# The remainder of 48 gated features as 32 and 16 rows in four row groups, and the last store on ScalarE's queue

## The chip, the core and the metric

The kernel runs on one core of a Trainium2 chip. The metric is the device time of one execution in microseconds (us). Five engines work in parallel and meet at semaphores: TensorE (PE in the profile; its weight loads are shown apart as PEld), VectorE (DVE), ScalarE (ACT), GpSimd (POOL) and SyncE (SP). SP, ACT and POOL also give out DMA transfers; each gives out its own in order, and an instruction that waits holds up all that is behind it on the same engine.

## What is computed

A layer-normed input feeds two branches, whose results are added to the input (S = 2048 tokens, D = 512, bf16):

```python
xn = layernorm(x)
# A: sliding window of 8 keys, two apart, 32 heads of 16
q, k, v = split(xn @ wqkv)
A = (softmax(q . k[s - 2 w] / 4 + mask) @ v) @ wo
# B: gated by a mix over the tokens, Fh = 688
z  = gelu(xn @ w_in);  z1, z2 = z[:, :688], layernorm(z[:, 688:])
g  = w_sp @ z2 + b_sp
B  = (z1 * g) @ w_out
out = x + A + B
```

The change concerns the last product, `(z1 * g) @ w_out`, which sums over 688 = 5 x 128 + 48 features, and how it shares TensorE with `... @ wo`.

## The kernel before

Tokens are cut into 16 tiles of 128, and into two halves `th` of 8 tiles. The order of work is written out by hand in two lists, `ten` (TensorE and ScalarE) and `vec` (VectorE), and a small function walks them and issues each step as soon as the steps that it needs have been issued. In these lists `M<j>` is the mix of tile j (`mix_tile`, matmuls on L378, moved out of PSUM by ScalarE on L381), `g<j>` its gate, `a<th>.<n>` a step of attention on VectorE (L351, L355, L364), `O<n>` a load of output weights, `X<th>` a load of the residual, `Q0`, `Q2`, `Q3` the output matmuls, and `F<n>` the end of a group of tiles.

**The gate.** `gate(j)` (L385) multiplies the mixed tile by `z1` on VectorE (L386) and gives out DMA transposes on SP's queue, which put the features on the partitions, in `uT`: chunks 0 to 4 are full, chunk 5 holds the remaining 48. Tiles whose `j // 2` is even take one transpose (L390), and the 48 rows land on partitions 0 to 47. The other tiles take two (L392, L393), the second so placed that the 48 rows land on partitions 64 to 111.

**The output matmuls.** TensorE can use its 128 rows as one group, as two of 64, or as four of 32, and matmuls in different groups can run at the same time; `tile_position=(row, 0)` picks the group. Tiles are grouped by four: group 0 is tiles 0, 2, 4, 6, group 1 is 1, 3, 5, 7, and 2 and 3 are the same for the second half. For each tile three kinds of matmul add up in one PSUM bank:

- `gated_full` (L417): five matmuls on all 128 rows.
- `gated_rest` (L423): one matmul of 48 rows, in the row group of 64 at row 0 or 64, so that neighbouring tiles of a group run in pairs.
- `attention_out` (L429; in the last group L566): for each of 16 head dimensions, four matmuls of 32 rows in the row groups 0, 32, 64 and 96, one for each tile of the group.

`out_pair` (Q0) does groups 0 and 1: full, rest, rest, attention, attention, full. `out_group(2)` (Q2) does full, rest, attention. `out_last(3)` (Q3) does attention, rest, full, and there the last tile is computed in two column halves in two banks, so that one half can be moved out while the other is computed.

**The end.** `finish` (L432) adds the residual on VectorE (L434) and stores the tile from SP's queue (L435). The two halves of tile 15 make the last two stores. `finish_pair` does two tiles with one store (L442).

**Loads in ScalarE's queue.** `load_wout` (L404, step O4) gives out three DMAs: the five full chunks of `w_out` (L405), and its last 48 rows twice, for partitions 0 and 64 (L407). `load_wo` (L402) loads `wo` in four steps. `load_res` (L410) loads the residual, that of the second half on SP, behind the transposes of tile 15.

Of the kernel before, what the change touches and what calls it, by code (L numbers as in the profile page):

```python
# [7 lines left out]
BF16 = mybir.dt.bfloat16  # L8
# [5 lines left out]
P = 128  # L14
S = 2048
D = 512
# [8 lines left out]
HS = S // 2  # L25
GS = HS // 4
FH = 688
F = 2 * FH
FHALF = FH // 2
MF = FH // P  # L30
FREST = FH - MF * P
# [7 lines left out]
def kernel(  # L39
# [14 lines left out]
    A = nc.scalar  # L54
    G = nc.gpsimd
    PE = nc.tensor
    SP = nc.sync
# [36 lines left out]
    qk_r = [sb.tile([P, QKH], BF16, name=f"qk{t}") for t in range(2)]  # L94
    qk = [r[:].rearrange("p (a c s) -> p a c s", a=2, c=C) for r in qk_r]
    uT = [r[:, 0:(MF + 1) * HS].rearrange("p (m s) -> p m s", m=MF + 1) for r in qk_r]
    gs = [qk_r[0][:, (MF + 1) * HS + n * FH:(MF + 1) * HS + (n + 1) * FH] for n in range(3)]
    prod = [sb.tile([P, 2 * C * HS], BF16, name=f"prod{n}")[:] for n in range(2)]
    z2_r = sb.tile([P, NT * FH], BF16, name="z2")
# [285 lines left out]
    def gate(j, g):  # L385
        V.tensor_tensor(z1u[:, j, 0:FH], g, z1u[:, j, 0:FH], ALU.mult)  # L386
        th, t0 = j // 8, (j % 8) * P

        if j // 2 % 2 == 0:
            SP.dma_start_transpose(uT[th][:, :, t0:t0 + P], z1u[:, j, :])  # L390
        else:
            SP.dma_start_transpose(uT[th][:, 0:MF, t0:t0 + P], z1u[:, j, 0:MF * P])  # L392
            SP.dma_start_transpose(uT[th][:, MF, t0:t0 + P], z1u[:, j, MF * P - 64:MF * P + 64])  # L393

    def idle(n, k=1):

# [6 lines left out]

    def load_wout():  # L404
        A.dma_start(wout[:, 0:MF, :], B_w_out[0:MF * P, :].rearrange("(m p) n -> p m n", p=P))  # L405
        for r in (0, 64):
            A.dma_start(wout[r:r + FREST, MF, :], B_w_out[MF * P:FH, :])  # L407

    def load_res(th):
        (SP if th else A).dma_start(xr[th], x2[th * HS:(th + 1) * HS, :].rearrange("(i p) d -> p i d", p=P))  # L410
# [5 lines left out]
        for m in range(MF):  # L416
            PE.matmul(po[:, cols], uT[th][:, m, t0:t0 + P], wout[:, m, cols], start=(start and m == 0), stop=(stop and m == MF - 1))  # L417

    def gated_rest(tiles, start, stop, bank=None, cols=slice(0, D)):
        for i in tiles:  # L420
            r, t0 = 64 * (i // 2 % 2), (i % 8) * P
            b = po[i] if bank is None else bank
            PE.matmul(b[:, cols], uT[i // 8][r:r + FREST, MF, t0:t0 + P], wout[r:r + FREST, MF, cols],  # L423
                      start=start, stop=stop, tile_position=(r, 0))

    def attention_out(th, s, pos, start, stop):
        for d in range(DH):
# [1 line left out]
                PE.matmul(pos[g], op[32 * g:32 * g + 32, th, d, s * P:(s + 1) * P], wo_r[32 * g:32 * g + 32, d, :],  # L429
                          start=(start and d == 0), stop=(stop and d == DH - 1), tile_position=(32 * g, 0))  # L430

    def finish(i, po, cols=slice(0, D)):  # L432
        o = nxt("ot", ot)
        V.tensor_tensor(o[:, cols], po[:, cols], xr[i // 8][:, i % 8, cols], ALU.add)  # L434
        SP.dma_start(out2[i * P:(i + 1) * P, cols], o[:, cols])  # L435

    def finish_pair(i):

# [10 lines left out]
    for i in range(5, NT):  # L449
# [4 lines left out]
        p01 p02 zs8 m10 zn8 zn9 zn10 zn11 p03 W1 f10 zs12 p10 zn12 zn13 zn14 zn15  # L454
        m11 d11 x0 m12 g0 d12 p11 u0 g1 m13 p12 W2 W3 f13 p13 c0 g2
        a0.0 a0.1 g3 x1 a0.2 a0.3 g4 a0.4 g5 a0.5 a0.6 a0.7 g6 u1 a0.8 g7 a0.9 g8 a0.10 g9 a0.11 c1 g10
        a1.0 a1.1 g11 a1.2 a1.3 g12 a1.4 g13 a1.5 g14 a1.6 a1.7 g15 X1 a1.8 a1.9 F0 a1.10 a1.11 F1 F2
    """.split()
    ten = """
        T0 T1 B GL z0 z1 h0 T3 h1 z2 h2 z3 h3 LZ k00 k01 q0 k02 q1 k03 q2 z4 h4 z5 q3 h5 k10 k12 k11 k13  # L460
# [75 lines left out]
    def out_pair():  # L536

        first, second = groups[0], groups[1]
        for i in first:
            gated_full(i, po[i], True, False)  # L540
        gated_rest(first, False, False)
        gated_rest(second, True, False)
        attention_out(0, 0, [po[i] for i in first], False, True)
        attention_out(0, 1, [po[i] for i in second], False, False)
        for i in second:
            gated_full(i, po[i], False, True)

    def out_group(n):
        tiles = groups[n]
        for i in tiles:  # L550
            gated_full(i, po[i], True, False)
        gated_rest(tiles, False, False)
        attention_out(n // 2, n % 2, [po[i] for i in tiles], False, True)

    def out_last(n):

        tiles = groups[n]
        th, s, last = n // 2, n % 2, tiles[-1]
        hb = [po[last], po[groups[n - 1][0]]]
        cols = [slice(0, D // 2), slice(D // 2, D)]  # L560
        for d in range(DH):
            for g in range(4):
                a = slice(32 * g, 32 * g + 32)
                for dd, b, c in [(d, po[tiles[g]], slice(0, D))] if g < 3 else \
                        [(2 * d % DH + x, hb[d // 8], cols[d // 8]) for x in range(2)]:
                    PE.matmul(b[:, c], op[a, th, dd, s * P:(s + 1) * P], wo_r[a, dd, c],  # L566
                              start=(dd == 0), stop=False, tile_position=(32 * g, 0))
        gated_rest(tiles[:3], False, False)
        for b, c in zip(hb, cols):
            gated_rest([last], False, False, b, c)  # L570
        for i in tiles[:3]:
            gated_full(i, po[i], False, True)
            finish(i, po[i])
        for b, c in zip(hb, cols):
            gated_full(last, b, False, True, c)
            finish(last, b, c)

    gates, done = {}, set()
    at = [attend(0), attend(1)]
# [1 line left out]
    def do(n):  # L581
        k, a = n[0], n[1:]
        i = int(a) if a.isdigit() else 0
        th, w2 = (int(a[0]), int(a[1])) if len(a) == 2 and a.isdigit() else (i, 0)
        if k == "T":
            turn_pe(i)
            if i == 0:
                idle(1)
        elif n[:2] == "zs":
            z2_stats(int(n[2:]), 4)  # L590
        elif n[:2] == "zn":
            z2_norm(int(n[2:]), False)
        elif n == "z0":

            gates["z0"], gates["z1"] = nxt("mm", mm), nxt("mm", mm)
            for t, hh in ((0, 0), (1, 0), (0, 1)):
                z_half(t, 1, gates[f"z{t}"], hh)
        elif n == "z1":
            turn_pe(2)
            z_half(1, 1, gates["z1"], 1)  # L600
        elif k == "z":
            gates[n] = z_part(i, 1)
        elif k == "h":
            z2_gelu(i, gates[f"z{i}"])
        elif k == "q":
            z2_square(i)
        elif k == "k":
            qk_chunks(th, w2 // 2, w2 % 2)
        elif k == "v":
            v_pair(i)  # L610
        elif k == "H":
            v_halo()
        elif k == "S":
            head_sum(th, w2)
        elif k == "B":

            pb = mm[2][:, 1, :].bitcast(BF16)[:, 0:NT]
            PE.transpose(pb, b16[:], ident[0:NT, 0:NT])
            A.copy(b_col[:], pb)
        elif k == "y":  # L620
            z1_tile(i)
        elif k == "M":
            gates[i] = mix_tile(i)
        elif k == "W":
            load_wsp(i)
        elif k == "O":
            load_wo(i) if i < 4 else load_wout()
        elif k == "X":
            load_res(i)
        elif n == "GL":  # L630
            A.preload_act_table(ACT.Gelu_apprx_tanh)
        elif n[:2] == "EG":
            A.preload_act_table(ACT.Gelu_apprx_tanh)
        elif n[:2] == "EL":
            A.preload_act_table_set("natural_log_exp_and_others")
        elif k == "Q":
            [out_pair, None, lambda: out_group(2), lambda: out_last(3)][i]()
        elif k == "F":
            tiles = groups[i]
            for t in (0, 2):  # L640
                if (i, t) in ((0, 0), (0, 2), (1, 0)):
                    finish_pair(tiles[t])
                else:
                    finish(tiles[t], po[tiles[t]])
                    finish(tiles[t + 1], po[tiles[t + 1]])
        elif k == "e":
            softmax_exp(i)
        elif k == "i":
            softmax_inv(i)
        elif k == "s":  # L650
            ln_stats(i)
        elif k == "R":
            ln_root_act(i, 1)
        elif k == "V":
            ln_inv(i)
        elif n == "LE":
            load_early()
        elif k == "r":
            ln_root(i, 1)
        elif k == "n":  # L660
            ln_norm(i)
        elif k == "t":
            turn_dma(i)
        elif n == "LZ":
            load_x(12, 4, A)
        elif n == "LX":
            load_tokens()
        elif n == "LW":
            load_weights()
        elif k == "m":  # L670
            run(prod_ops(th, w2)[0])
        elif k == "j":
            run(prod_ops(th, w2)[1])
        elif k == "f":
            prod_ops(th, w2)[2]()
        elif k == "p":
            prod_ops(th, w2)[3]()
        elif k == "d":
            fold_dma(th, w2)
        elif k == "K":  # L680
            k_halo()
        elif k == "x":
            run(softmax_max(i))
        elif k == "u":
            run(softmax_sum(i))
        elif k == "c":
            run(softmax_scale(i))
        elif k == "g":
            gate(i, gates[i])
        elif k == "a":  # L690
            at[int(a[0])][int(a[2:])]()
        done.add(n)
# [53 lines left out]
```

## Time and profile before

| | us |
|---|---|
| median of three runs (201.41, 201.60, 201.67) | 201.6 |
| the profiled execution, its own time | 201.44 |
| its span in the trace | 199.7 |
| PE busy | 195.2 (98%) |
| DVE busy | 175.7 (88%) |
| ACT busy | 95.0 (48%) |
| POOL busy | 39.0 (20%) |

All durations below are from the one profiled execution. Its span is 1.7 us shorter than its time; the difference lies outside the trace. PE's share is high in any case, because matmuls are pipelined and their recorded ends are modelled: what counts is the distance from the start of one matmul to the start of the next. The output stage starts at 162.7 us; VectorE's last work ends at 196.98 us. The granted clock of TensorE is full in all slices of the span.

### The profile page before, as it was taken

Reading aid. Unit: us, or ns where it says so; the run is one execution under the profiler, and the core shown is the slowest. Engines: PE = TensorE matmul, PEld = TensorE weight load, DVE = VectorE, ACT = ScalarE, POOL = GpSimd, SP = SyncE. Lnnn points to the kernel's source line nnn. Section 1 sums busy time; section 2 is a strip of 40 time slices with the busy share of each in tenths; the row PEclk is TensorE's granted clock in tenths of the full one; section 3 lists DMA queues with packets and bytes.
Section 4 is the critical chain, followed back from the end, with each engine's and each line's share of the span. In section 5 each row is a group of like instructions: output and inputs, shape, how many; then the busy total and the mean of one; then the engine's idle time right before and its main releaser. Section 6 shows DMA issues by size and latency. Waiting matters only on the chain.

```text
span 199.7 us, 3843 instructions
## 1 busy us (share of the span) xinstructions
PE 195.2 (98%) x1587; PEld 119.0 (60%) x1587; DVE 175.7 (88%) x192; ACT 95.0 (48%) x149; POOL 39.0 (20%) x62
## 2 busy tenths in 40 slices
PE   7999999999999999999999999999999999999993
PEld 2655555555666666666566666666666654444652
DVE  4899689999889799999999999999999799897333
ACT  3779879899888738886433373312221110000000
POOL 4367540149490421600000000000000000000000
PEclk9999999999999999999999999999999999999999
DMA  6999679599640837898979199996959711712023
GB/s 173 290 261 182 108 161 289 113 199 198 133 83 17 196 62 151 173 112 81 236 173 213 26 266 289 111 278 134 260 101 249 141 43 39 257 61 105 9 99 105
DMA packets 64289, 30.84 MB, mean 154 GB/s; under 512 B 53440, under 2 KB 62512, under 8 KB 64144
## 3 DMA queue, kind: packets, MB, share of 16 engines
q1 hardware_dynamic: 59296, 19.23, 46.1%
q0 software_dynamic: 1904, 6.59, 16.9%
q10 hardware_dynamic: 3072, 4.78, 9.3%
q8 instruction: 12, 0.20, 0.4%
q14 instruction: 5, 0.04, 0.1%
HBM read 10.03 MB, written 2.10 MB: 61 GB/s over the span
## 4 chain that ended last, share of the span: by engine, by line
PE 95%; DVE 1%; DMA 1%; ACT 0%; issue 0%
PE mm L378 37%; PE mm L213 19%; PE mm L258 14%; PE mm L273 7%; PE mm L417 7%; PE mm L429 5%; PE aux L417 2%; PE mm L566 1%; DMA z<-in_A_x_dram 1%; PE mm L423 1%; PE aux L309 1%; DVE stats L186 1%; PE aux L205 0%; PE aux L566 0%; ACT xnT L206 0%; DVE z L434 0%
## 5 line engine op out<-in xcount | busy, mean ns | idle before, releaser
L378 PE MATMUL mm<-z,wsp 128*128 128x344 bf16 x384 | 56.8, 309 | 0.0
L378 PEld LDWEIGHTS <-wsp 128*128 128x128 bf16 x384 | 37.5, 98 | 18.8 <-issue 0.4
L213 PE MATMUL mm<-wts,xnT 128*128 128x344 bf16 x256 | 40.3, 309 | 0.2 <-ACT xnT L206 0.2
L381 ACT ACTIVATE qk<-mm,b_col 128x688 bf16<-128x688 f32 x16 | 13.3, 833 | 49.8 <-PE mm L378 46.0
L351 DVE TENSOR_TENSOR prod<-vp,a_sb 128x4096 bf16<-128x4096 bf16 x16 | 36.0, 2283 | 0.0
L213 PEld LDWEIGHTS <-xnT 128*128 128x128 bf16 x256 | 24.7, 98 | 13.9 <-ACT xnT L206 0.5
L258 PE MATMUL mm<-xnT,wts 128*128 128x512 bf16 x128 | 29.1, 379 | 0.0
L355 DVE TENSOR_TENSOR prod<-prod,prod 128x8192 bf16<-128x8192 bf16 x6 | 26.5, 4419 | 0.1
L293 DVE TENSOR_TENSOR prod<-qk 128x4096 bf16<-128x4096 bf16 (+1 forms) x12 | 22.7, 1930 | 1.4 <-ACT qk L260 1.4
L258 PEld LDWEIGHTS <-wts 128*128 128x128 bf16 x128 | 14.6, 114 | 11.9
L378 PE MATMUL mm<-z,z 128*128 128x344 bf16 x128 | 19.2, 309 | 0.0
L260 ACT CAST qk<-mm 128x1024 bf16<-128x1024 f32 x16 | 16.2, 1012 | 4.8 <-PE mm L258 3.8
L378 PEld LDWEIGHTS <-z 128*128 128x128 bf16 x128 | 12.5, 98 | 6.1
L417 PE MATMUL mm<-wts,qk 128*128 128x512 bf16 (+1 forms) x65 | 14.7, 371 | 0.0
L273 PE MATMUL mm<-xnT,wts 128*32 128x512 bf16 x256 | 14.2, 379 | 0.0
L250 ACT ACTIVATE z<-mm 128x688 bf16<-128x688 f32 x16 | 11.8, 744 | 4.5 <-PE mm L213 4.5
L417 PEld LDWEIGHTS <-qk 128*128 128x128 bf16 x85 | 8.1, 98 | 9.2 <-issue 0.6
L186 DVE BATCH_NORM_STATS2 stats<-z 128x6 f32<-128x512 bf16 x16 | 11.0, 685 | 2.0 <-DMA z<-in_A_x_dram 1.9
L224 ACT ACTIVATE z<-mm 128x688 bf16<-128x688 f32 x16 | 11.9, 745 | 1.6 <-PE mm L213 1.6
L229 ACT ACTIVATE z_junk<-z 128x688 bf16<-128x688 bf16 x16 | 12.4, 773 | 0.0
L273 PEld LDWEIGHTS <-wts 128*32 128x32 bf16 x256 | 9.5, 138 | 4.3
L434 DVE TENSOR_TENSOR z<-mm,wsp 128x512 bf16<-128x512 f32 (+1 forms) x7 | 4.3, 649 | 8.0 <-PE mm L429 4.8
(98 smaller groups left out, 210.1 us busy)
## 6 DMA issues: line engine op xcount, KB each, us to landing
prod<-prod POOLq DMA_DIRECT2D x6, 512.0 KB, 5.1
z<-z POOLq DMA_DIRECT2D x4, 512.0 KB, 5.9
wts<-in_A_wo_dram ACTq DMA_DIRECT2D x4, 512.0 KB, 6.0
out_dram<-z SPq DMA_DIRECT2D x9, 128.0 KB, 1.7
z<-in_A_x_dram SPq DMA_DIRECT2D x4, 256.0 KB, 4.3
wts<-in_A_wqkv_dram SPq DMA_DIRECT2D x2, 512.0 KB, 6.6
z<-in_A_x_dram ACTq DMA_DIRECT2D x1, 1024.0 KB, 6.6
wsp<-in_A_x_dram SPq DMA_DIRECT2D x1, 1024.0 KB, 5.6
```

The lines of the kernel that those rows point to most:

```text
L186: V.bn_stats(stats[:, i, :], xs[:, i, :])
L213: PE.matmul(pz[:, hh, 0:FHALF], xnT[:, kc, i * P:(i + 1) * P], w_z2[:, hh, kc] if part else w_z1[:, kc, hh * FHALF:(hh + 1) * FHALF], star ...
L229: A.activation(z2_junk[:], z2[:, i, :], ACT.Square, accum_out=zsq[:, i:i + 1])
L258: PE.matmul(pq[:, cc, :], w_c[:, kc], xnT[:, kc, t0:t0 + D], start=(kc == 0), stop=(kc == C - 1))
L260: A.copy(qk[b // 2][:, a, 2 * c2:2 * c2 + 2, o:o + D], pq[:])
L273: PE.matmul(pv[32 * g:32 * g + 32, dd, :], w, r, start=(kc == 0), stop=(kc == C - 1), tile_position=(0, 32 * g))
L293: ops.append(lambda ww=ww, k=k, c=c: V.tensor_tensor(pr[:, ww, c], q[:, c], k[:, c], ALU.mult))
L351: return lambda: V.tensor_tensor(dst, vp[:, :, th, off:off + GS], a_sb[:, th, w].unsqueeze(1).broadcast_to([P, DH, GS]), ALU.mult)
L355: return lambda: V.tensor_tensor(dst, dst, x, ALU.add)
L378: PE.matmul(pg[:, hh, 0:FHALF], w[:, k, (j % 2) * P:(j % 2 + 1) * P], z2[:, k, hh * FHALF:(hh + 1) * FHALF], start=(k == 0), stop=(k == NT ...
L381: A.activation(g.rearrange("p (a b) -> p a b", a=2), pg[:, :, 0:FHALF], ACT.Identity, bias=b_col[:, j:j + 1])
L417: PE.matmul(po[:, cols], uT[th][:, m, t0:t0 + P], wout[:, m, cols], start=(start and m == 0), stop=(stop and m == MF - 1))
```

## The change

- `gate` gives out one transpose for each tile; the 48 rows always land on partitions 0 to 47 of chunk 5.
- A new step `spread_rest`, behind the gates of tiles 7, 9, 11, 13 and 15, copies pieces of the 48 rows between partitions by DMA: for the tile pair g = 0 to 3 of a half, 32 features to the row group 32 g and the other 16 to the same row group in a second buffer (for g = 1 the two buffers change places). Two of the eight pieces of a half lie where they must already. So there are six copies for the first half, on POOL's queue behind gate 7, and six for the second, on SP's queue, two by two or one by one behind gates 9, 11, 13 and 15.
- `gated_rest` does two matmuls for each tile, of 32 and of 16 rows, in the same row group of 32: first the 32 rows of all four tiles, then the 16 rows.
- `load_wout` loads the weight rows that belong to them: five DMAs on ACT's queue in place of three, and three more on POOL's.
- The residual of the second half is asked for behind gate 13 in place of gate 15.
- The last store, that of the second half of tile 15, is given out by ACT's queue in place of SP's.

```diff
+    uB = [qk_r[1][:, (MF + 1 + n) * HS:(MF + 2 + n) * HS] for n in range(2)]
+    wB = sb.tile([P, D], BF16, name="wB")
...
     def gate(j, g):
         V.tensor_tensor(z1u[:, j, 0:FH], g, z1u[:, j, 0:FH], ALU.mult)
         th, t0 = j // 8, (j % 8) * P
-        if j // 2 % 2 == 0:
-            SP.dma_start_transpose(uT[th][:, :, t0:t0 + P], z1u[:, j, :])
-        else:
-            SP.dma_start_transpose(uT[th][:, 0:MF, t0:t0 + P], z1u[:, j, 0:MF * P])
-            SP.dma_start_transpose(uT[th][:, MF, t0:t0 + P], z1u[:, j, MF * P - 64:MF * P + 64])
+        SP.dma_start_transpose(uT[th][:, :, t0:t0 + P], z1u[:, j, :])
...
     def load_wout():
         A.dma_start(wout[:, 0:MF, :], B_w_out[0:MF * P, :].rearrange("(m p) n -> p m n", p=P))
-        for r in (0, 64):
-            A.dma_start(wout[r:r + FREST, MF, :], B_w_out[MF * P:FH, :])
+        last, first = B_w_out[MF * P + 32:FH, :], B_w_out[MF * P:MF * P + 32, :]
+        A.dma_start(wout[0:FREST, MF, :], B_w_out[MF * P:FH, :])
+        A.dma_start(wout[64:96, MF, :], first)
+        G.dma_start(wout[96:P, MF, :], first)
+        G.dma_start(wB[32:64, :], first)
+        for r, q in ((0, G), (64, A), (96, A)):
+            q.dma_start(wB[r:r + FREST - 32, :], last)
...
-    def gated_rest(tiles, start, stop, bank=None, cols=slice(0, D)):
-        for i in tiles:
-            r, t0 = 64 * (i // 2 % 2), (i % 8) * P
-            b = po[i] if bank is None else bank
-            PE.matmul(b[:, cols], uT[i // 8][r:r + FREST, MF, t0:t0 + P], wout[r:r + FREST, MF, cols],
-                      start=start, stop=stop, tile_position=(r, 0))
+    def rest_of(i, x):
+        g, t0 = i % 8 // 2, i % 8 * P
+        rows = slice(32 * g, 32 * g + (FREST - 32 if x else 32))
+        if (x == 0) != (g == 1):
+            return rows, uT[i // 8][rows, MF, t0:t0 + P], wout[rows, MF]
+        return rows, uB[i // 8][rows, t0:t0 + P], wB[rows]
+
+    def gated_rest(tiles, start, last=None):
+        for x in range(2):
+            for i in tiles:
+                rows, u, w = rest_of(i, x)
+                for b, c in last if last and i == tiles[3] else [(po[i], slice(0, D))]:
+                    PE.matmul(b[:, c], u, w[:, c], start=(start and x == 0), stop=False, tile_position=(rows.start, 0))
+
+    def spread_rest(th, g):
+        t = slice(2 * g * P, 2 * (g + 1) * P)
+        for x in range(2):
+            dst = (uT[th][:, MF] if (x == 0) != (g == 1) else uB[th])
+            n, r = (FREST - 32, 32) if x else (32, 0)
+            if (g, x) not in ((0, 0), (1, 1)):
+                (SP if th else G).dma_start(dst[32 * g:32 * g + n, t], uT[th][r:r + n, MF, t])
...
-        for b, c in zip(hb, cols):
+        for b, c, q in zip(hb, cols, (SP, A)):
             gated_full(last, b, False, True, c)
-            finish(last, b, c)
+            finish(last, b, c, q)
...
             gate(i, gates[i])
+            if i in (7, 9, 11, 13, 15):
+                for g in range(4) if i == 7 else [(i - 9) // 2]:
+                    spread_rest(i // 8, g)
```

## The prediction on record

> **What bounds the kernel now.** I read the chain that ended last first, because busy shares say little here. By engine it is
>
> ```profile
> PE 95%; DVE 1%; DMA 1%; ACT 0%; issue 0%
> ```
>
> so from the first microseconds to the end, time goes only where one matmul follows another; only the head and the last VectorE step with its store lie outside. A transfer or a ScalarE step that is off this chain is worth nothing until it makes a matmul wait. Next, the chain in the second output group (start, us, engine, tile, line, count):
>
> ```profile
> 182.87 1.08 PE mm L417 x5
> 183.95 0.54 PE mm L423 x4
> 184.49 0.53 PE mm L429 x5
> ```
>
> Five full matmuls take 1.08, that is 0.216 each. The four rest matmuls run in two pairs; two rounds at 0.216 would be 0.432, and they take 0.54. The missing 0.11 is seen in the timeline of PE there:
>
> ```profile
> 183.57 0.38 PE L417 MATMUL mm<-wts,qk 128*128 128x512 bf16 x1
> 183.88 0.39 PE L423 MATMUL mm<-wts,qk 48*128 48x512 bf16 x2
> 184.11 0.38 PE L423 MATMUL mm<-wts,qk 48*128 48x512 bf16 x2
> 184.42 0.40 PE L429 MATMUL mm<-wts,xnT 32*128 32x512 bf16 x4
> 184.65 0.39 PE L429 MATMUL mm<-wts,xnT 32*128 32x512 bf16 x4
> ```
>
> Read the starts. From the last full matmul (128 rows) to the first pair (groups of 64) is 0.31, from pair to pair 0.23, from the last pair to the first four of attention (groups of 32) 0.31 again, then 0.23. Within one way of grouping the step is 0.216. So each **change of row grouping** costs (0.31 - 0.216) + (0.23 - 0.216) = 0.11. The row of four also shows that four matmuls of 32 rows start at once. Last, the end: VectorE, then SP's queue.
>
> ```profile
> 196.08 0.41 DVE L434 TENSOR_TENSOR z<-aux,wsp 128x256 bf16<-128x256 f32 x1
> 196.56 0.42 DVE L434 TENSOR_TENSOR z<-mm,wsp 128x256 bf16<-128x256 f32 x1
> ```
> ```profile
> 195.11 0.33 SPq L435 DMA_DIRECT2D out_dram<-z  x1
> 196.19 0.33 SPq L435 DMA_DIRECT2D out_dram<-z  x1
> 196.61 0.38 SPq L435 DMA_DIRECT2D out_dram<-z  x1
> 197.09 0.40 SPq L435 DMA_DIRECT2D out_dram<-z  x1
> ```
>
> The store at 195.11 follows its VectorE step (194.39 + 0.69 = 195.08) by 0.03, that at 196.19 (195.47 + 0.69) by 0.03. The last one follows 196.98 by 0.11: SP was giving out the store before it until 196.99.
>
> **The matmuls.** The rounds stay. Q0: before 8 rest matmuls in pairs, 4 rounds; after 16 in fours, 4 rounds. Q2: 4 in 2 rounds, then 8 in 2. Q3: 3 whole and 2 half-wide ones in 2 rounds, then 10 in 2. What goes is one change of grouping in each place: Q0 and Q2 went 128, 64, 32 and go 128, 32; Q3 went 32, 64, 128 and goes 32, 128. That is 3 x 0.11 = **0.33 us** on the path. The trace has no change from 128 to 32 on the rows. From 128 to 64 is 0.31, 64 to 32 is 0.31, and the way back from attention to full in Q0 (32 to 128) is 0.30 (174.84 to 175.14); so I take one change at the same price. At worst it costs as much as the two it replaces, and the gain is 0; were it free, the gain would be 0.66. The 17 added matmuls are hidden in the rounds: attention in Q3 (L566) has five in a round, two of them half-wide, at the same step (187.88, 188.10, 188.31). Added semaphore waits on weight loads are met long before; Q0 has ten such waits around its rest now, Q2 half as many, and both show the same gaps of 0.31.
>
> The page TensorEngine Tiling (Array Packing) of the Trainium skill, section Instruction Overhead, speaks against the change: it puts about 60 cycles of overhead on each matmul, and 17 of them at its 2.4 GHz would be an estimated 0.43 us, which would use up the gain. The trace disagrees where matmuls run in fours: the starts of the four above carry one time, and the round is no longer than that of one full matmul.
>
> **The end.** On ACT's queue, idle by then, the last store need not wait for SP. It can start 0.03 after VectorE instead of 0.11: 0.08 gained. ACT's nearest row is its residual load, whose semaphore is met at 148.94 and which starts at 149.03, 0.09 behind: 0.02 gained. I take 0.05; the ends are 0.08 gained and, if ACT's issue (0.32 to 0.53 in its rows, against 0.40) is as slow as its slowest, 0.11 lost. Landing (1.6 to 1.8 for stores) stays.
>
> **Loads in ACT's queue.** Two more DMAs at 0.48 (L407, 433 to 534 ns) put off the table load (117.79), the exp behind it and the move out of tile 6 (L381, 121.00) by 1.0, to 121.0 + 1.0 + 0.83 = 122.8. Its first reader is VectorE's gate at 123.51, and TensorE wants the bank three tiles later, at 130. Hidden by 0.7; if VectorE did slip, it has 1.27 idle before its gate at 159.14, and its last attention step ends at 180.93 where matmuls ask for it at 184.42.
>
> **SP's queue.** Eight second transposes go (1.23 each); six copies come. Each pair of copies waits for the landing of transposes given out just before, and behind it wait the transposes of the next two tiles, the residual and, last, the stores. By medians: gate 15's transpose goes out at 166.77, lands 4.5 later (L390) at 171.3; two copies at 0.5 are out by 172.3 and land 1.7 (stores) to 5.4 (POOL's accumulating copies) later, by 177.7. They are wanted in the second rest round of Q2, at about 184.0. Hidden by 6.3. The stores of group 0, ready from 173.0, wait for nobody's benefit: the output buffers have 12 places. The residual is first read at 188.09.
>
> **POOL's queue.** It is idle from 84. Gate 7's transpose goes out at 141.60 and lands 4.5 to 9.3 later, by 150.9; six copies at 0.87 (L302) are out by 156.1 and land 5.4 later, at 161.5; wanted at 167.4. Hidden by 5.9. The copies that move least alike are those of the value halos, and they are slow (rows of the DMA issues):
>
> ```profile
> vp<-vp POOLq DMA_DIRECT2D x1, 96.0 KB, 11.7
> ...
> b<-in_B_b_sp_dram POOLq DMA_DIRECT2D x1, 4.0 KB, 3.8
> ...
> vp<-vp POOLq DMA_DIRECT2D x1, 16.0 KB, 11.1
> ```
>
> They move pieces of 32 bytes; the new copies move 16 or 32 pieces of 512 bytes, which is nearer to the small load. I keep 11.7 for the rival.
>
> **Sum.** 201.44 - 0.33 - 0.05 = 201.06. The profiled execution is 0.16 under the median of 201.6; from the median the same sum gives 201.22. I predict the middle, **201.1**. A measurement of this kernel tells about 0.2% (0.4 us) from no change, and the gain of 0.38 sits on that line.
>
> **Rivals.**
>
> 1. *Nothing is left of it*: a change from 128 to 32 is as dear as the two changes before, or the added matmuls cost time in line, and ACT gives out no sooner. 201.4 to 201.6. For it: no row shows that change. Against it: three kinds of change have one price. Chance 0.08. The page's 60 cycles end here too.
> 2. *The copies come late* (slower). The place is SP's queue, where every copy holds up the next transposes. If every transpose takes L392's largest landing, 6.5, a pair of gates takes 1.25 + 6.5 and its copies 0.5 each; from 146.2 that gives 154.5, 162.7, 171.5, the residual to 172.0, and 180.7 for the last copies, which land 5.4 later at 186.1, 2.1 behind 184.0: 201.06 + 2.1 = 203.2. With the halo's 11.7 it would be 8 late. On POOL, 10.0 for six issues at the halo's 1.67 and 11.7 to land end at 172.6. It decides when the last copy lands after 184.0 (SP) or 167.4 (POOL). Against it: the 6.5 has several transposes in flight, while a queue that waits has few, and the transposes at 166.77 and 168.04 landed in 2.4. Chance 0.10.
> 3. *Pieces run in pairs, not fours*: 8 more rounds at 0.216, 1.73: 202.8. Against it: L429 and L566. Chance 0.04.
>
> The page SBUF — State Buffer of the Trainium skill, section SBUF: two separate sides, warns of copies from POOL's queue: their descriptors can wait for VectorE. It names two-port operations, and VectorE runs two-input ones in this stretch; beside such ones (L293, 72 to 84 us) POOL's issues took 0.84 to 0.93. By that rule rival 2 would decide on POOL rather than on SP.
>
> **From these to the numbers.** The forecast has 0.78, and by the line at 0.4 us it splits: 0.50 faster and 0.28 within. Rival 1 adds 0.07 to within and 0.01 to slower, rivals 2 and 3 add 0.14 to slower. Faster 0.50, same 0.35, slower 0.15. Range: the unknown prices give 201.06 - 0.33 - 0.03 = 200.7 to 201.06 + 0.33 + 0.16 = 201.55 from the profiled execution, 0.16 more from the median: 200.7 to 201.7. It takes in rival 1 and leaves out 2 and 3.
>
> **What the changed profile would show.** The rest line at 0.43 + 0.11 with fours at one time, and one step of 0.31 in each place, not two; PE's output stage shorter by 0.33; the last store on ACTq within 0.05 of VectorE's end; no DMA named before a rest weight load. I am wrong if a first step from 128 to 32 is over 0.40, if fours come apart, or if PE idles before the rest.

## The result, and the profile after

The changed kernel takes 200.93 us (median of six runs, 200.64 to 200.97) against 201.52 for the kernel before; the ratio is 0.9972, with a 95% interval of 0.9961 to 0.9983, that is 0.56 us faster (0.34 to 0.79). The forecast was 0.38 faster, at 201.1. Ratios here and below leave out a single execution of `e2_rest_only` (208.05), which fell in a slower state that its other eleven do not show.

The profiled execution took 200.74, its span 199.0. Cut into three, the two profiles differ so:

| us | before | after | difference |
|---|---|---|---|
| start to the first full matmul of the output stage | 162.74 | 162.54 | -0.20 |
| from there to the end of VectorE's last step (output stage) | 34.24 | 33.94 | -0.30 |
| from there to the span's end (the end) | 2.75 | 2.53 | -0.22 |

The chain that ended last still runs through TensorE alone:

```profile
PE 95%; DVE 1%; DMA 1%; issue 0%; ACT 0%
```

In it, the rest of Q2 (now on L436; full is L421, attention L449) takes what it took, but for twice the matmuls, and the attention behind it takes 0.10 less. The last line of the chain is, before:

```profile
184.49 3.56 PE mm L429 x64
```

and after, with the rest ahead of it:

```profile
183.65 0.55 PE mm L436 x8
184.20 3.46 PE mm L449 x64
```

The starts in PE's timeline show why:

```profile
183.28 0.38 PE L421 MATMUL mm<-wts,qk 128*128 128x512 bf16 x1
183.59 0.39 PE L436 MATMUL mm<-wts,qk 32*128 32x512 bf16 x2
183.82 0.38 PE L436 MATMUL mm<-wB,qk 16*128 16x512 bf16 x2
184.03 0.38 PE L449 MATMUL mm<-wts,xnT 32*128 32x512 bf16 x4
```

From 128 rows to 32 is 0.31, as the other changes of grouping were; then comes a step of 0.23, and from the rest to attention 0.21 where 0.31 had been: no change of grouping there any more. The rows of the two rest rounds show two of their four matmuls; the other two start within 0.01 of them. Counted from the first full matmul, the matmuls behind the rest come 0.10 earlier in Q0, 0.20 in Q2 and 0.30 in Q3: each of the three places gives 0.10. At the end, VectorE and the queues (start, duration):

```profile
195.57 0.41 DVE L454 TENSOR_TENSOR z<-aux,wsp 128x256 bf16<-128x256 f32 x1
196.06 0.42 DVE L454 TENSOR_TENSOR z<-mm,wsp 128x256 bf16<-128x256 f32 x1
```
```profile
196.11 0.39 SPq L455 DMA_DIRECT2D out_dram<-z  x1
```
```profile
196.51 0.38 ACTq L455 DMA_DIRECT2D out_dram<-z  x1
```

ACT gives out the last store at 196.51, 0.03 after VectorE is done at 196.48; SP, busy with the store before until 196.50, would not have given out the next at once: in the kernel before it was done with one at 196.99 and gave out the next at 197.09.

### The profile page after: what moved, and what is told of

The parts are those of the page before. It is cut to its first block, busy times and chain, and to the rows that moved or that the text cites. A ratio compares the mean times of both kernels' runs of the same rounds, so it can differ in the third digit from the quotient of the medians.

```text
span 199.0 us, 3881 instructions
## 1 busy us (share of the span) xinstructions
PE 193.7 (97%) x1597; PEld 119.0 (60%) x1604; DVE 175.6 (88%) x192; ACT 95.0 (48%) x149; POOL 43.5 (22%) x71
## 4 chain that ended last, share of the span: by engine, by line
PE 95%; DVE 1%; DMA 1%; issue 0%; ACT 0%
PE mm L382 38%; PE mm L217 19%; PE mm L262 14%; PE mm L277 7%; PE mm L421 7%; PE mm L449 5%; PE aux L421 2%; PE mm L586 1%; DMA z<-in_A_x_dram 1%; PE mm L436 1%; PE aux L313 1%; DVE stats L190 1%; PE aux L209 0%; PE aux L586 0%; ACT xnT L210 0%
## 5 line engine op out<-in xcount | busy, mean ns | idle before, releaser
L421 PE MATMUL mm<-wts,qk 128*128 128x512 bf16 (+1 forms) x62 | 14.2, 370 | 0.4 <-issue 0.3
L444 POOL DMA_DIRECT2D qk<-qk x6 | 3.0, 500 | 49.9 <-DMA wB<-in_B_w_out_dram 27.8
L421 PEld LDWEIGHTS <-qk 128*128 128x128 bf16 x85 | 8.2, 98 | 9.2 <-issue 0.6
```

## The experiments

Two theories stood at the start. For the output stage: three changes of row grouping are gone, at about 0.1 each. For the end, which gained 0.22 where 0.05 was forecast: its parts are 0.07 from VectorE's end to the store's issue (0.104 to 0.032), 0.02 in the landing (1.601 to 1.580), and 0.13 in what I call the **closing exchange**, from the landing of the last store to the span's end (1.040 to 0.913), in which all engines exchange semaphores. The first theory for that last part was that ScalarE, idle since 163 us, is slow to wake. The rivals: it is chance of one execution, or it has to do with the program. The 0.20 of the head also needed telling apart from the change. All kernels in one table (us; the time is the median of the timed runs, or one run). Times from different sets of runs are not to be compared: the kernel before took 201.37 beside e1 to e4, 201.50 beside e5 to e8 and 201.55 beside e9 to e12; the ratios below are taken within a set.

| kernel | first full matmul | output stage | the end | closing exchange | time |
|---|---|---|---|---|---|
| before | 162.74 | 34.24 | 2.75 | 1.04 | 201.52 |
| after | 162.54 | 33.94 | 2.53 | 0.91 | 200.93 |
| e1_tail_only | 162.57 | 34.24 | 2.54 | 0.92 | 201.11 |
| e2_rest_only | 162.48 | 33.94 | 2.63 | 0.91 | 201.14 |
| e3_act_awake | 162.78 | 33.94 | 2.64 | 0.92 | 200.96 |
| e4_regroup4 | 162.48 | 34.37 | 2.53 | 0.91 | 201.35 |
| e5_before_again | 163.02 | 34.24 | 2.74 | 1.04 | 201.71 |
| e6_before_awake | 163.51 | 34.24 | 2.90 | 0.91 | 201.59 |
| e7_regroup8 | 162.71 | 34.80 | 2.53 | 0.92 | 201.86 |
| e8_copies_f1 | 162.93 | 41.39 | 2.54 | 0.92 | 207.70 |
| e9_before_two_more | 163.24 | 34.24 | 2.62 | 0.91 | 201.39 |
| e10_before_awake2 | 162.65 | 34.24 | 2.84 | 0.92 | 201.61 |
| e11_copies_f0 | 163.11 | 33.94 | 2.53 | 0.92 | 201.32 |
| e12_no_16 | 163.20 | 33.06 | 2.54 | 0.92 | 200.50 |

The output stage repeats within 0.01 between executions; the head does not: it lies anywhere from 162.48 to 163.51, with kernels of both kinds in both halves of that span. All of that lies ahead of the matmuls of the mix, which start anywhere from 70.62 to 71.58; from there to the first full matmul it is 91.87 in every kernel but e6 (91.94). So the 0.20 of the head is not shown to belong to the change, and the stages, not the total times, carry the verdicts.

**One part alone.**

```diff
 # e1_tail_only: the kernel before
-        for b, c in zip(hb, cols):
+        for b, c, q in zip(hb, cols, (SP, A)):
             gated_full(last, b, False, True, c)
-            finish(last, b, c)
+            finish(last, b, c, q)
 # e2_rest_only: the changed kernel
-        for b, c, q in zip(hb, cols, (SP, A)):
+        for b, c, q in zip(hb, cols, (SP, SP)):
```

> The kernel before, with nothing changed but the queue of the last store: ACT in place of SP. Theory: the end got shorter by 0.22 us in three places (0.07 from VectorE's end to the store's issue, 0.02 in its landing, 0.13 in the closing exchange of the engines, where ScalarE, asleep since 163 us, came last before), so 201.3 us against 201.5, and the time from VectorE's end to the span's end goes from 2.75 to 2.53. Rival: only the queue counts and the rest is chance of one execution, then 0.05 to 0.09, and the closing exchange stays as long as before.

Measured: ratio 0.9982 (0.9971 to 0.9993) to the kernel before; the end 2.54, output stage unchanged. All three parts of the 0.22 are there: issue 0.032, landing 1.579, closing exchange 0.924. The rival that only the queue counts falls.

> The changed kernel with its last store on SP as before. Theory: three changes of row grouping are gone, the output stage (first full matmul to VectorE's end) is 0.31 to 0.33 us shorter than before, 201.2 us against 201.5, and the end is as before, 2.75. Rival: the first 116 us, which were 0.20 shorter in the one profiled execution, are shorter because of the change (moved buffers), then 201.0 and the matmuls of the mix start 0.2 earlier here too.

Measured: ratio 0.9981 (0.9969 to 0.9993); output stage 33.94, exactly the changed kernel's. So the 0.30 comes from the row groups alone. The mix starts at 70.62, which is the sign that the rival asked for; but it starts at 70.71 in e1, where no buffer moved, and anywhere from 70.62 to 71.33 in the other kernels with the moved buffers, so this sign decides nothing. The end is 2.63, not 2.75: the issue is late again by 0.10 and the landing 1.61, yet the closing exchange is 0.91 with a ScalarE that slept from 163 us on. So either part alone brings the 0.13 of the exchange, and the gains of e1 and e2 may not be added.

**What wakes ScalarE?**

`finish` now also returns its tile, and `junk` is a new buffer of one column:

```diff
 # e3_act_awake: the kernel e2; e6 and e10: the kernel before
         for i in tiles[:3]:
             gated_full(i, po[i], False, True)
-            finish(i, po[i])
+            o = finish(i, po[i])
+        A.copy(junk[:], o[:, 0:1])      # e10: into zbias[:, 0:1]
```

> As the kernel with the last store on SP, plus one ScalarE copy of a single column that waits for the last whole tile of VectorE, about 1 us before the end. Theory that ScalarE is late in the closing exchange because it was asleep: the exchange gets 0.13 us shorter, the queue's 0.07 is not gained: 0.13 below the kernel without the copy. Rival that the DMA on ACT's queue itself does it: no change.

Measured: closing exchange 0.92, as without the copy; the ratio to the kernel before is 0.9977 (0.9964 to 0.9989), within the interval of e2. There was nothing left to gain, so this run could not decide. It took the kernel before itself:

> The kernel before, profiled once more. The closing exchange (from the last store's landing to the span's end) was 1.04 us in its first profile and 0.91 to 0.92 in the four others, also where ScalarE slept (the changed kernel with its last store on SP). If it belongs to the program it is 1.04 again; if it is chance of one execution, 0.91. The output stage must be 34.24 again; the matmuls of the mix start anywhere in 70.6 to 70.9, by when the granted clock became full, if the head is chance.

Measured: 1.04 again, with the output stage 34.24. It belongs to the program. The mix started at 71.15, outside the 70.6 to 70.9 that were expected: the head scatters more than was thought. In the rows of the kernel's last line, ScalarE's DRAIN is the one that differs (e5, then e9, which is told below):

```profile
L741 ACTq EVENT_SEMAPHORE  x2: 17/17/17, 199.3 to 199.9; - x2
L741 ACTq DRAIN  x1: 128/128/128, 199.7 to 199.7; - x1
```
```profile
L743 ACTq EVENT_SEMAPHORE  x2: 17/17/17, 199.5 to 200.0; - x2
L743 ACTq DRAIN  x1: 14/14/14, 199.6 to 199.6; - x1
```

In e5 it comes 0.39 behind ScalarE's first semaphore there and takes 128 ns; in e9, 0.09 and 14 ns. In e5 the next semaphore of POOL comes 0.03 behind the end of this DRAIN, though POOL's own DRAIN ended 0.16 before; in e9 it comes 0.04 behind POOL's own. By this order, in e5 the last semaphores wait for ScalarE.

> The kernel before plus the one-column ScalarE copy about 1 us before the end. If the long closing exchange of the kernel before comes from a ScalarE that sleeps, it is 0.91 here and the time 0.13 below the kernel before; if it was chance, the time is that of the kernel before within 0.05.

Measured: closing exchange 0.91, but the ratio is 1.0006 (0.9994 to 1.0018): nothing gained. The end is even longer, 2.90, as the last store took 1.88 to land. This could be the profile's execution, or the new buffer; so once more without a new buffer:

> The kernel before plus the one-column ScalarE copy about 1 us before the end, this time into a column of a buffer that the kernel has already, so that no buffer moves. Closing exchange 0.91 as with the moved buffer; time 0.13 below the kernel before. If the time is that of the kernel before again, the 0.13 of the closing exchange does not reach the device time.

Measured: closing exchange 0.92, end 2.84, time 201.61 against 201.55 in the same runs (ratio 0.9986, 0.9956 to 1.0015: open; three of those 21 runs of the kernel before took 203.7 to 204.0). The landing is long again, 1.81. In the DMA rows of the last microseconds, e10 has an instruction load among its stores (first the queue, with packets, MB and share of the 16 engines, then the two half stores, with KB and us to landing), where the kernel before has none:

```profile
q14 instruction: 1, 0.01, 0.8%
...
out_dram<-z SPq DMA_DIRECT2D x2, 64.0 KB, 2.0
```

Its single packet of 8 KB runs from 197.35 to 197.91 in e10, 198.22 to 198.87 in e6, both while the last two stores land. In the kernel before it runs at 200.04, after the span; in e1 at 198.45, after the last landing; in the changed kernel, e2 and e9 at 159 to 160. So the copy also seems to have moved an instruction load into the last stores' way: 0.13 gained, 0.21 to 0.28 lost.

```diff
 # e9_before_two_more: the kernel before
     def load_wout():
...
+        for n in range(2):
+            A.copy(zbias[:, n:n + 1], eps_t[:])
```

> The kernel before plus two one-column ScalarE copies in the middle, at about 117 us, where the changed kernel has two more DMAs in ScalarE's queue; nothing new near the end. If the long closing exchange depends on where ScalarE's last instructions fall in its program, it is 0.91 here too and the time 0.13 below the kernel before. If only a ScalarE that does something late shortens it, it is 1.04.

Measured: closing exchange 0.91 with nothing new near the end; 201.39 against 201.55, ratio 0.9986 (0.9963 to 1.0009). So the theory of sleep falls as stated: two more ScalarE instructions at 117 us do the same. All twelve kernels with the short exchange give ScalarE more copies or DMAs than the kernel before. The 8 KB load comes at 200.0 in the kernel before, at 197.3 to 198.5 with one more (e1, e6, e10), and at 159 to 162 with two or more. This fits a theory that the place where ScalarE's program ends decides; but no kernel here changes another engine and leaves ScalarE's program as it was, so it is argued and not shown. Whether it is the load itself that ScalarE waits for stays open: its packet in the kernel before is recorded after the wait. The total times of e9 and e10 are too scattered to show 0.13 by themselves.

**The price of a change of grouping.** The same matmuls in another order:

```diff
 # e4_regroup4: the changed kernel, in Q0 and Q2; e7_regroup8 with tiles[:2], and one more full tile behind the 16 rows
-        for i in tiles:
+        for i in tiles[:3]:
             gated_full(i, po[i], True, False)
-        gated_rest(tiles, False)
+        # 32 rows of all four (the last tile's bank starts here), full of the last tile, 16 rows of all four
+        gated_rest(tiles, False, own=tiles[3:], mid=tiles[3:])
```

> The changed kernel with the same matmuls, but in Q0 and in Q2 the five full matmuls of the group's last tile are moved between the 32-row and the 16-row pieces, so that the row grouping changes four times more (128, 32, 128, 32 in place of 128, 32, twice). Theory: 4 x 0.11 = 0.43 us more than the changed kernel. Rival, that the gain came from something else in the rest matmuls than from the changes of grouping: no more than 0.1.

> The changed kernel with eight more changes of row grouping: in Q0 and Q2 the full matmuls of the last two tiles are moved behind the 32-row and behind the 16-row pieces. With a fixed price for each change, 8 x 0.108 = 0.86 us longer in the output stage than 33.94, that is 34.80; the rival, that part of the 0.43 of the four changes came from the moved full matmuls, gives another slope than twice the 0.43.

Measured: 34.37 and 34.80, that is 0.43 and 0.86 over the changed kernel, 0.108 for each change of grouping, on a straight line through both. In total time e4 gives up nearly the whole gain (ratio to the kernel before 0.9996, 0.9984 to 1.0008), and e7 has none of it left (1.0012, 1.0000 to 1.0024). The chain of e4 in Q2 shows the four pieces:

```profile
182.73 0.33 PE mm L436 x4
183.06 1.18 PE mm L421 x5
184.24 0.33 PE mm L436 x4
184.57 3.46 PE mm L451 x64
```

A round of four is 0.33 where 0.216 is work, and five full matmuls take 1.18 where they took 1.08. Both rivals fall: 0.43 is not 0.1, and the slope is the same.

**The late copies.** In the changed kernel the last copies on SP go out at 171.27 and 171.86, and land 1.7 to 1.8 later, ten microseconds before they are used. Two kernels move the six copies of the second half behind stores on SP's queue:

```diff
 # e11_copies_f0 and e8_copies_f1; Q2 waits for the new step Y
-        ... a1.9 F0 a1.10 a1.11 F1 F2
+        ... a1.9 F0 Y a1.10 a1.11 F1 F2      # e11
+        ... a1.9 F0 a1.10 a1.11 F1 Y F2      # e8
+        elif k == "Y":
+            for g in range(4):
+                spread_rest(1, g)
```

> The changed kernel with the six copies of the second half given out on SP behind the first group's stores, so from about 174.8 to 178 us, landing by 180, 4 us later than in the changed kernel but before 184. By the late-copies rule this costs nothing: output stage 33.94. If waiting copies cost TensorE something before that point, more.

Measured: output stage 33.94. The last copy goes out at 178.19 in place of 171.86, and these six microseconds cost nothing:

```profile
175.00 3.77 SPq L444 DMA_DIRECT2D qk<-qk  x6
```

Its single time of 201.32 has a head 0.57 longer than the changed kernel's.

> The changed kernel with the six copies of the second half given out late: on SP behind the stores of the first half's last tiles, so from about 183.4 us, each 0.5, landing 1.7 later. The late-copies rival's rule, that lateness counts from 184.0 on and one for one: the last copy goes out at 186.0 to 186.4 and lands at 187.7 to 188.1, so TensorE stalls before or in the rest of Q2 and the time grows by 3.7 to 4.1 us. If TensorE does other work first or the copies' waits do not bind there, less than 1.

Measured: 207.70, ratio to the kernel before 1.0291 (1.0264 to 1.0319); output stage 41.39, 7.4 over the changed kernel in the profile. The copies went out from 183.84 to 187.6. TensorE waited in the rest, as the rule said: for the fifth copy until 188.22 and for the last until 188.79, so that attention starts 4.4 late (the head is 0.39 longer here, so it was due at 184.42). The expected 3.7 to 4.1 was missed all the same. The other part of the loss is in the windows (PE busy, PEld, DVE, ACT, POOL, granted clock, DMA share, GB/s):

```profile
183.40:188.20 4.80, 1.73 (x6) 0.37 (x4) 0.01 (x1) 0.00 (x0) 0.00 (x0) 0.96 0.32 105
188.20:195.50 7.30, 7.28 (x77) 2.78 (x81) 0.18 (x1) 0.00 (x0) 0.00 (x0) 0.56 0.01 3
195.50:200.00 4.50, 4.34 (x89) 3.51 (x83) 2.30 (x4) 0.00 (x0) 0.00 (x0) 1.00 0.33 117
```

From 187.78 on the granted clock is at half for 6.83 us, and attention takes 6.3 where it took 3.5. The 4.4 us late, the 2.9 of the slower clock and 0.2 more in the last group are, but for rounding, the 7.4; one microsecond of lateness cost 1.7 in this execution. It is the slowest of four (208.56; the others 207.13, 207.20 and 208.19), and the two quicker ones list a granted clock of 0.991 in place of 0.983, an estimated half of the time at half clock: the price varies. The Trainium skill's page TensorE: Matmul & The Clock Gate, Part 1, states that an idle window of about 3.4 us halves the clock until a busy window opens it again. The trace agrees in time, with 3.8 us from the first rest matmul to the fall of the clock and a half clock for 6.83; but TensorE was not wholly idle in it: three matmuls ran, and the longest gap was 2.0 us.

**The price of a round.**

```diff
 # e12_no_16: the changed kernel
-        for x in range(2):
+        for x in range(1):
```

> The changed kernel without the 16-row matmuls: the last 16 of the 688 gated features are left out of the result. One round of four goes in each of the four groups: 4 x 0.216 = 0.86 us less in the output stage, 33.08, if a round of four pieces of 16 rows is on the path as a full matmul is. Rival, that small pieces are partly hidden behind others: less than 0.86.

Measured: output stage 33.06, 0.88 less: 0.22 for each round of four. The 16-row pieces cost a full round each and no more.

## Why the prediction was right, point by point

- **What bounds it**: right. Nothing that was added to the queues made TensorE wait: the chain is 95% PE in both, and from the mix to the first full matmul both take 91.87.
- **Three changes of grouping, 0.33**: right. 0.302 measured between the kernels, 0.108 for each in e4 and e7. The unknown change from 128 to 32 costs what its neighbours cost, 0.31 to the next start (the way from 32 back to 128 is 0.316 in the trace, and not 0.30). The rival that nothing is left of it falls.
- **The rounds stay, and 17 matmuls more cost nothing**: right. Eight rest matmuls take 0.55 where four took 0.54. The 0.43 us that were estimated from the Trainium skill's page TensorEngine Tiling (Array Packing) are not seen.
- **The end, 0.05**: the mechanism was right for its part, and the size of the term was off. The store starts 0.032 behind VectorE, a gain of 0.072, near the better of the two ends that were given; with the landing it is 0.09. The other 0.13 was no term of the sum at all: what stands behind the last landing was taken as fixed, and in the kernel before it holds a wait for ScalarE that the changed kernel does not have. With 0.30 and 0.22 the sum is 0.52, and the measured ratio gives 0.56. The range held the time, and the forecast was 0.17 too slow, mostly for this reason. That this unforeseen quarter of the gain had the sign of the forecast is luck.
- **Loads in ACT's queue**: right, hidden. The table load moved from 117.79 to 118.82, tile 6 was moved out by 122.75, forecast 122.8.
- **SP's queue**: right, hidden by 10 rather than 6.3. The last copy goes out when it was forecast (done at 172.45, forecast 172.3), but lands 1.7 after its issue, and not 5.4. The thought that transposes land sooner in a queue that waits is not borne out: their median is 5.2, where those of L390 had 4.5.
- **POOL's queue**: hidden, but the working was too pessimistic. The six copies do not all wait for gate 7: they go out when their own pair has landed, the first at 95.0, the last at 147.4. They were taken at 0.87 and cost 0.50 beside VectorE's two-input operations, so no wait of POOL's descriptors for VectorE is seen here:

```profile
L444 POOL DMA_DIRECT2D qk<-qk x6: 494/499/507, 95.0 to 147.4; - x6
L444 SPq DMA_DIRECT2D qk<-qk x6: 516/567/608, 149.2 to 171.9; - x6
```

- **Rival 2, late copies**: its place and its point of decision were right (free at 180, dear at 188), its price of one for one was too low by the part that the clock added. The condition did not arise: the copies were ten microseconds early.
- **Rival 3, pairs instead of fours**: falls, with pieces of 16 rows as with 32: four start within 0.01.

## What to carry to other kernels

Count the changes of TensorE's row grouping in the order of the matmuls, and price one from the starts around it (here 0.108 us): a remainder that is cut to the grouping of its neighbours costs the same rounds and fewer changes. Where work is put in a queue that must wait, find the point from which the wait counts; here a stall of 4.4 us cost 7.4, because the clock fell. Read the span behind the last store too; it is not a constant.

## What was not expected of the hardware

The closing exchange of the engines is 1.04 us in the kernel before, in both its profiles, and 0.91 to 0.92 in the twelve other kernels; two instructions more in the middle of ScalarE's program go with the shorter one. An instruction load of 8 KB that falls among the last stores goes with a landing of 1.81 to 1.88 in place of 1.58 to 1.61. Both together would explain why a ScalarE copy that shortens the exchange lengthened the end in e6 and e10; that the load causes either is argued from where it lies, and not shown. Last, the clock fell to half in e8 though no gap between matmuls ahead of it was longer than 2.0 us.
